# Attention and two expert layers on one core: zero products in TensorE's waits, other chunk widths, a mask copied by VectorE, pooled keys in a tile of their own, and a new written order

## The chip, the cores and the metric

The kernel runs on one core of one Trainium2 chip. The metric is the device time of one execution in microseconds (us). The times shown are the median of three runs and the three runs themselves; the profile is of a further execution with a time of its own.

## The reference, cut to what matters

Inputs are fp32: q, k and v of 2 x 8 heads, 576 positions, 64 wide. The output is 1152 x 512.

```python
def _attn_ref(q, k, v):
    ...
    q_d = q.reshape(B, H, Sd, factor, D).mean(axis=3)      # factor 4: 144 pooled positions; k_d, v_d alike
    ...
    out_d = sm_attn(q_d, k_d, v_d)
    out_up = np.repeat(out_d, factor, axis=2)
    mask = np.abs(pos[:, None] - pos[None, :]) < factor    # a band of 7 keys
    scores = np.where(mask, scale * np.matmul(q, k.transpose(0, 1, 3, 2)), -1000000000.0)
    ...                                                    # softmax
    return out_up + np.matmul(attn, v)

def _moe_ref(x, w_in, w_out):                              # 1152 x 512, 512 x 2048, 2048 x 512
    h = x @ w_in
    g = h * (1.0 / (1.0 + np.exp(-h)))
    return g @ w_out

def _moe2_ref(x, domain_probs, w1, w2):                    # 4 experts, 512 x 1024, 1024 x 512
    p = domain_probs / (domain_probs.sum(-1, keepdims=True) + 1e-09)
    for e in range(E):
        out += p[:, e:e + 1] * (np.maximum(x @ w1[e], 0.0) @ w2[e])
```

## The kernel before, in words

Every large product is made of three: each factor is split into a high part in TensorE's rounded fp32 format and a low part, and high x high, high x low and low x high are added in PSUM. So a weight passes through a raw tile (DMA), a high part (ScalarE) and a low part (GpSimd or VectorE) before TensorE may use it. The weights of the first layer come as pairs of 32-bit halves in 64-bit places: step A (L236, ScalarE) scales the upper halves into a tile `dec`, step B (L239, VectorE) or Z (L242, ScalarE) shifts the lower bits, step C (L244, VectorE) joins them, step w (L250, ScalarE) makes the high part and step L (L251, GpSimd) the low part. There are 8 units of 4 such pieces (A0 to A31 and so on); units 0, 1, 4, 5 are of w_in, 2, 3, 6, 7 of w_out.

Attention is cut into 16 jobs of two heads and 256 or 320 positions. The steps of job i are: S (local scores and the mask, L403 and L410, TensorE), x (maximum and subtraction, L418 and L419, VectorE), e (exponential, L424, ScalarE), D (pooled scores, L444 for jobs 0 to 3 and L448 for the others, TensorE), n and d (their maximum and exponential), u, r and g (sums, reciprocals and scaling), T (transpositions, L490 and L492, TensorE) and a (their copies, L493 to L500, ScalarE), V (values, L518 and L522, TensorE), o and f (both outputs joined), h and l (the split of x into xh and xl). The keys of the first four jobs are pooled by GpSimd (k, L342), in place; those of later jobs with their queries (p). The mask, two unit matrices and two zeroed tiles for queries are made by GpSimd at the start (`constants`).

The first layer follows: G steps (x times w_in) and H steps (times w_out), over four chunks of positions and two halves of the 2048 hidden columns. In the first half the chunks are 256, 320, 256 and 320 wide (`XN`), in the second 256, 256, 256 and 384. The first two chunks of the first half are computed in quarters, woven with attention (`quarter`); the first products of all are M0 to M3 (`start_mm`, L993). Then come the four experts.

Each engine works its list in order. The order of the attention and of most of the first layer is written out by hand for each engine in `WRITTEN` (step names in a row); what is not named there, all of the experts among it, is put in order by the framework's scheduler. All loads go out on SP's queue, also in written order. Eight transfers are under way at most: each later one waits for the one eight before it, or for its own tile to be free.

Of the kernel before, what the change touches and what calls it, by code (L numbers as in the profile page):

```python
# [22 lines left out]
NT = NB * S  # L23
# [31 lines left out]
LOW_ON_DVE = (0, 1, 2, 3)  # L55
# [7 lines left out]
def attention_moe_kernel(ctx, tc, kqa, kqb, qtl, va, vb, w64, w1d, w2d, dpr, out):  # L63
# [28 lines left out]
    const.tile([128, 16], F32, name="gap_w")  # L92
    prt = const.tile([128, 9, NE + 1], F32, name="pr")
# [132 lines left out]
    def split_raw(u, j, t):  # L226
        if u < 8:
# [4 lines left out]
            d = d_p.tile([128, 512], F32, tag="dec", name="dec")  # L232
# [19 lines left out]
        else:  # L252
# [5 lines left out]
            behind(ACT, ACT.activation(out=h[:, c], in_=t, func=ACTF.Copy))  # L258
            behind(DVE, DVE.tensor_tensor(out=l[:, c], in0=t, in1=h[:, c].bitcast(F32), op=ALU.subtract))
# [17 lines left out]
    def eye(t):  # L277
        return (POOL.memset(t, 0.0), POOL.affine_select(out=t, in_=t, compare_op=ALU.not_equal, fill=1.0, base=0,
                                                        pattern=[[-1, 128]], channel_multiplier=1))

    def constants():
        mark("cm", POOL.memset(mask, 0.0))
        for h in range(2):
            m = mask[64 * h:64 * h + 64]
            mark("cm", POOL.affine_select(out=m, in_=m, pattern=[[0, 6], [1, WIN]], compare_op=ALU.is_ge,
                                          fill=NEG, base=0, channel_multiplier=-1),
                 POOL.affine_select(out=m, in_=m, pattern=[[0, 6], [-1, WIN]], compare_op=ALU.is_ge,
                                    fill=NEG, base=6, channel_multiplier=1))
# [193 lines left out]
    def trans(j):  # L482
# [5 lines left out]
        j.at = ac.tile([WIN, 5, 128], F32, tag="at", name="at")  # L488
        for m in range(nb):
# [19 lines left out]
    def values(j):  # L509
# [3 lines left out]
        v = vd[b, hp]  # L513
        for h in range(2):
# [145 lines left out]
    def quarter(ci, p, o, n):  # L660
        c = slice(o, o + n)
        g = [4 * ci + i for i in range(4)]
        two = n == 256
# [9 lines left out]
        if two:  # L673
            b = [mm_tile() for _ in range(2)]
            groups = [[(d, half(b[d // 2], d % 2)) for d in range(4)]]
        else:
            groups = [[(d, mm_tile()) for d in ds] for ds in ((0, 1, 2), (3,))]
        step[0] -= 0.5
        for sums in groups:
            first = {}  # L680
            for i in range(4):
                wh, wl = parts(2 + p, i)
                for d, ps in sums:
                    if not two or len(sums) == 4:
                        next_step(0.125)
                    s = slice(d * 128, d * 128 + 128)
                    h, l = gh[g[i]][:, 0:n], gl[g[i]][:, 0:n]
                    for x, (a, y) in enumerate(((wh, h), (wh, l), (wl, h))):
                        z = two and d % 2
                        m = PE.matmul(out=ps[:, 0:n], lhsT=a[:, s], rhs=y, start=(not z and i == 0 and x == 0),  # L690
                                      stop=(i == 3 and x == 2), skip_group_check=True)
                        if i == 0 and x == 0:
                            first[d] = m
                            if z:
                                after(m, first[d - 1])
                        mark(f"H{ci}_{d}_{4 * p + i}", m)
                if i:
                    attn_tick()
            for d, ps in sums:
                ya = acc[:, d * NT + o:d * NT + o + n]  # L700
                if p == 0:
                    i = ACT.activation(out=ya, in_=ps[:, 0:n], func=ACTF.Copy, scale=0.5)
                else:
                    i = DVE.scalar_tensor_tensor(out=ya, in0=ps[:, 0:n], scalar=0.5, in1=ya, op0=ALU.mult, op1=ALU.add)
                mark(f"ya{ci}_{d}_{p}", i)
# [34 lines left out]
    def stage_ahead():  # L740
        while todo and not pieces:
# [156 lines left out]
    def outputs(e, ci, ch, p):  # L898
# [303 lines left out]
```

## Time and profile before

| | us |
|---|---|
| median of 3 runs | 652.15 |
| the three runs | 652.35, 652.15, 647.56 |
| the profiled execution, device time | 649.48 |
| its span, first to last instruction | 647.70 |

In the profile TensorE is busy for 629.0 us (97%), VectorE for 415.4, ScalarE for 325.3 and GpSimd for 249.1. A busy TensorE is not yet one at its peak: the granted clock and the number of matmuls in a stretch have to be read beside it. A matmul's own duration overlaps that of the next, so its cost in a stream is the stretch divided by the number of matmuls that begin in it. The time ahead of the first instruction and behind the last, 649.48 - 647.70 = 1.78 us, lies outside the span.

### The profile page before, as it was taken

What the parts mean: (1) busy time and instruction counts of PE and PEld (TensorE: products, weight loads), DVE (VectorE), ACT (ScalarE), POOL (GpSimd) and SP (SyncE); (2) the same over time, 40 slices, a digit from 0 to 9 for tenths busy, and PEclk for the clock granted to TensorE, in tenths of its full rate; (3) what the DMA queues carried; (4) which work ended last, traced back from release to release, by engine and by line L of the source; (5) the groups of instructions that cost most, each with busy time, mean ns of one, the idle gap of its engine ahead of it and who ended that gap; (6) DMA issues with size and microseconds to landing.
All of it is one profiled execution on the core that took longest, in us unless ns stands there. A gap on an engine that the chain in (4) does not pass through costs nothing.

```text
span 647.7 us, 13723 instructions
## 1 busy us (share of the span) xinstructions
PE 629.0 (97%) x5492; PEld 617.6 (95%) x5492; DVE 415.4 (64%) x859; ACT 325.3 (50%) x746; POOL 249.1 (38%) x353
## 2 busy tenths in 40 slices
PE   4989999999999999999999999999999999999995
PEld 3779999999999999999999999999999999999995
DVE  5878676547445737756668954769855579755534
ACT  2788776578725525443346533355533366433321
POOL 7567532034400004443646412654433564333210
PEclk9789999999999999999999999999999999999998
DMA  8955551235600400420013300024200020001001
GB/s 276 285 164 187 175 173 56 78 100 163 194 2 1 132 1 1 162 67 2 1 34 108 113 9 1 1 67 131 66 1 2 1 66 1 1 33 35 2 32 50
DMA packets 16928, 48.17 MB, mean 74 GB/s; under 512 B 2976, under 2 KB 4256, under 8 KB 16864
## 3 DMA queue, kind: packets, MB, share of 16 engines
q1 hardware_dynamic: 16864, 47.29, 23.4%
q8 instruction: 43, 0.70, 0.5%
q14 instruction: 21, 0.17, 0.1%
HBM read 44.93 MB, written 2.36 MB: 73 GB/s over the span
## 4 chain that ended last, share of the span: by engine, by line
PE 94%; DVE 3%; ACT 2%; DMA 1%; issue 0%; POOL 0%; ACTq 0%
PE mm L603 57%; PE p L864 27%; PE mm L690 4%; PE s L403 2%; PE o L522 1%; PE t L490 1%; PE o L518 1%; DVE acc L892 1%; DMA kq<-in_kqa_dram 1%; PE mm L993 1%; PE s L410 1%; PE s L448 0%; PE t L492 0%; ACT dec L236 0%; PE mm L403 0%
## 5 line engine op out<-in xcount | busy, mean ns | idle before, releaser
L603 PE MATMUL mm<-xh,wbuf 128*128 128x256 f32 (+2 forms) x1248 | 259.6, 292 | 0.0
L603 PEld LDWEIGHTS mm<-xh,wbuf 128*128 128x128 f32 x1248 | 203.7, 188 | 0.1
L603 PE MATMUL mm<-xl,wbuf 128*128 128x256 f32 (+2 forms) x624 | 182.0, 292 | 0.0
L849 POOL TENSOR_TENSOR r<-r 128x128 f32<-128x128 f32 x160 | 95.0, 606 | 177.4 <-ACT r L843 133.1
L852 DVE TENSOR_TENSOR h<-r,h 128x384 fp32r<-128x384 f32 (+1 forms) x128 | 91.6, 718 | 65.7 <-ACT h L851 65.4
L851 ACT ACTIVATE h<-r 128x384 fp32r<-128x384 f32 (+1 forms) x128 | 73.3, 578 | 93.5 <-POOL r L849 54.5
L603 PEld LDWEIGHTS mm<-xl,wbuf 128*128 128x128 f32 x624 | 117.1, 188 | 0.0
L864 PE MATMUL p<-wext,h 128*128 128x256 f32 x672 | 89.2, 276 | 0.0
L864 PE MATMUL p<-wbuf,h 128*128 128x256 f32 x672 | 82.7, 276 | 0.0
L864 PEld LDWEIGHTS p<-wext,h 128*128 128x128 f32 x672 | 82.2, 188 | 0.0
L864 PEld LDWEIGHTS p<-wbuf,h 128*128 128x128 f32 x672 | 79.4, 188 | 0.0
L603 PE MATMUL mm<-gh,wbuf 128*128 128x256 f32 (+2 forms) x384 | 77.1, 292 | 0.0
L603 PEld LDWEIGHTS mm<-gh,wbuf 128*128 128x128 f32 x384 | 62.0, 188 | 0.0
L843 ACT ACTIVATE r<-mm 128x512 f32<-128x512 f32 x48 | 28.6, 596 | 65.4 <-PE mm L603 64.7
L849 DVE TENSOR_TENSOR r<-r 128x128 f32<-128x128 f32 x96 | 39.3, 410 | 34.0 <-ACT r L843 29.4
L603 PE MATMUL mm<-gl,wbuf 128*128 128x256 f32 (+2 forms) x192 | 55.8, 291 | 0.0
L631 DVE TENSOR_TENSOR gl<-gf,gh 128x256 fp32r<-128x256 f32 (+2 forms) x64 | 34.2, 540 | 18.1 <-ACT gh L630 17.7
L625 DVE SCALAR_TENSOR_TENSOR gf<-th,mm 128x256 f32<-128x256 f32 (+2 forms) x64 | 28.7, 451 | 23.6 <-ACT th L624 21.6
L251 POOL TENSOR_TENSOR wbuf<-dec,wbuf 128x512 fp32r<-128x512 f32 x24 | 31.0, 1301 | 26.4 <-ACT wbuf L250 20.4
L892 DVE SCALAR_TENSOR_TENSOR acc<-p,pr,acc 128x256 f32<-128x256 f32 (+1 forms) x63 | 36.1, 605 | 3.6 <-PE p L864 3.0
L794 POOL TENSOR_TENSOR wext<-kst,wext 128x512 fp32r<-128x512 f32 x8 | 10.4, 1300 | 69.5 <-ACT wext L792 46.9
L630 ACT ACTIVATE gh<-gf 128x256 fp32r<-128x256 f32 (+2 forms) x64 | 28.0, 442 | 16.5 <-DVE gf L625 15.7
(173 smaller groups left out, 1035.2 us busy)
## 6 DMA issues: line engine op xcount, KB each, us to landing
stg<-in_w_dram SPq DMA_DIRECT2D x29, 512.0 KB
kst<-in_w2d_dram SPq DMA_DIRECT2D x16, 512.0 KB
kst<-in_w1d_dram SPq DMA_DIRECT2D x12, 512.0 KB
kq<-in_kqb_dram SPq DMA_DIRECT2D x8, 323.0 KB
kq<-in_kqa_dram SPq DMA_DIRECT2D x6, 419.0 KB
stg<-in_w1d_dram SPq DMA_DIRECT2D x4, 512.0 KB
acc<-in_w_dram SPq DMA_DIRECT2D x3, 512.0 KB
vw<-in_vb_dram SPq DMA_DIRECT2D x8, 180.0 KB
```

Of the source, the lines that this page charges most:

```text
L251: mark(f"L{4 * u + j}", POOL.tensor_tensor(out=l, in0=d, in1=h.bitcast(F32), op=ALU.subtract))
L603: ins = [PE.matmul(out=ps, lhsT=l, rhs=r, start=(first and i == 0), stop=(last and i == n - 1)) for i, (l, r) in enumerate(pairs)]
L625: mark(f"gf{c}_{ft}", DVE.scalar_tensor_tensor(out=gf[:, 0:n], in0=th[:, 0:n], scalar=1.0, in1=ps[:, 0:n], op0=ALU.add, op1=ALU.mult))
L630: latest[ACT] = mark(f"gh{c}_{ft}", ACT.activation(out=gh[g][:, 0:n], in_=gf[:, 0:n], func=ACTF.Copy))
L631: latest[DVE] = mark(f"gl{c}_{ft}", DVE.tensor_tensor(out=gl[g][:, 0:n], in0=gf[:, 0:n], in1=gh[g][:, 0:n].bitcast(F32), op=ALU.subtract))
L690: m = PE.matmul(out=ps[:, 0:n], lhsT=a[:, s], rhs=y, start=(not z and i == 0 and x == 0), stop=(i == 3 and x == 2), skip_group_check=True)
L843: ACT.activation(out=r[:, 0:4].rearrange("p s t -> p (s t)"), in_=ps[:, 0:512], func=ACTF.Relu)
L849: latest[eng] = eng.tensor_tensor(out=r[:, o], in0=r[:, a], in1=r[:, b], op=op)
L851: ACT.activation(out=h, in_=r[:, part], func=ACTF.Copy)
L852: latest[DVE] = DVE.tensor_tensor(out=l, in0=r[:, part], in1=h.bitcast(F32), op=ALU.subtract)
L864: ins = [PE.matmul(out=ps, lhsT=x, rhs=y, start=(opens and k == 0 and i == 0), stop=(k == 3 and i == n - 1), skip_group_check=True) for i, ...
L892: DVE.scalar_tensor_tensor(out=o, in0=ps, scalar=p, in1=o, op0=ALU.mult, op1=ALU.add)
```

## The change

- Matmuls on a tile of zeros (128 x 128 weights, 256 columns, bf16) are put ahead of three steps of TensorE: 3 ahead of S0, 11 ahead of T1 and 3 ahead of T2. They write a PSUM tile that the step then overwrites.
- The first half has the chunks of the second: 256, 256, 256, 384. The quarters keep their width of 256, and the code for 320 is gone. The tiles for 384 are opened ahead of the last chunk of the first half.
- One sixth of the mask is made by GpSimd on 70 columns; VectorE copies it to the others. The zeroing of the mask, unit matrices and query tiles goes from GpSimd to VectorE.
- The keys of jobs 0 to 3 are pooled through a tile `ktmp` and no longer in place.
- Step Z of units 4 to 7 (16 pieces) becomes step B on VectorE, and `dec` of these pieces lies in place in the raw tile.
- All five written orders are new and reach further, to chunk 5 and the first weights of the experts.

```diff
-XN = (256, 320, 256, 320)
-CHUNKS = (tuple(zip(XOFF, XN)), ((0, 256), (256, 256), (512, 256), (768, 384)))
+CHUNKS = ((0, 256), (256, 256), (512, 256), (768, 384))
+FILL = {"S0": 3, "T1": 11, "T2": 3}
-LOW_ON_DVE = (0, 1, 2, 3)
+LOW_ON_DVE = (0, 1, 2, 3) + tuple(range(16, 32))
+    ktmp = const.tile([128, SD, 2], F32, name="ktmp")
...
-            d = d_p.tile([128, 512], F32, tag="dec", name="dec")
+            d = d_p.tile([128, 512], F32, tag="dec", name="dec") if u < 4 else v[:, :, 1].bitcast(F32)
...
+    zeros = acc[:, 4470:4598].bitcast(BF16)
+
+    def fill(name, t):
+        for _ in range(FILL.get(name, 0)):
+            mark(name, PE.matmul(out=t, lhsT=zeros[:, 0:128], rhs=zeros, start=True, stop=True, skip_group_check=True))
+
     def constants():
-        mark("cm", POOL.memset(mask, 0.0))
+        mark("cw", DVE.memset(zeros, 0.0))
+        m1 = mask[:, 1]
+        mark("zcm", DVE.memset(m1, 0.0))
         for h in range(2):
-            m = mask[64 * h:64 * h + 64]
-            mark("cm", POOL.affine_select(out=m, in_=m, pattern=[[0, 6], [1, WIN]], compare_op=ALU.is_ge,
...
+            m = m1[64 * h:64 * h + 64]
+            mark("cm", POOL.affine_select(out=m, in_=m, pattern=[[1, WIN]], compare_op=ALU.is_ge, fill=NEG, base=0,
...
+        mark("cM", DVE.tensor_copy(out=mask[:, 0], in_=m1),
+             DVE.tensor_copy(out=mask[:, 2:6], in_=m1.unsqueeze(1).to_broadcast([128, 4, WIN])),
+             DVE.memset(mask[:, 0, 0:3], NEG), DVE.memset(mask[:, 5, WIN - 3:WIN], NEG))
...
-            mark(f"k{j.i}", fold(k4), padd(kd[j.b, j.hp], k4[:, :, 0], k4[:, :, 1]))
+            mark(f"k{j.i}", padd(ktmp, k4[:, :, 0:2], k4[:, :, 2:4]), padd(kd[j.b, j.hp], ktmp[:, :, 0], ktmp[:, :, 1]))
...
+            if hf == 0 and lastc:
+                m1ctx.close()
+                open_g(384)
...
-        """in_kq0 in_kq1 in_s0 in_kq2 in_vg0 in_kq3 in_vg1 in_kq4 in_kq5 in_vw0 in_s1 in_qt in_vg3 in_vw1 in_s3 in_vg2 in_vw2
+        """in_kq0 in_kq1 in_s0 in_vg0 in_s1 in_kq4 in_kq2 in_vg1 in_vw0 in_kq5 in_kq3 in_s2 in_vw1 in_qt in_vw2 in_s3 in_vg2
...
-        """S0 S1 D0 D1 S2 S3 T0 D2 S4 V0 S5 T1 D3 D5 D4 V1 M0 T2 M1 V2 T3 tD S6 T4 V3 D6 S7 M2 tT M3 V4 T5 D7 S8 T6 V5 D8
+        """S0 S1 D0 D1 T0 S4 S2 V0 S5 D2 S3 T1 D5 V1 D3 D4 T2 M0 T3 V2 M1 tD S6 T4 V3 D6 M2 S7 tT M3 V4 S8 T5 D7 H0_0_0
...
```

TensorE, from the first pooled scores (D0 and D1, L444) to the first values. Before:

```order
L444 MATMUL s<-kd,qp 64x144 x4
L403 MATMUL mm<-kq_f 64x70 x8
L410 LDWEIGHTS ident_103
L410 MATMUL mm<-mask,ident_103 128x280
L403 MATMUL mm<-acc 64x70 x8
L410 LDWEIGHTS ident_103
L410 MATMUL mm<-mask,ident_103 128x280
L490 MATMUL t_309<-ident,sm 70x128 x4
L492 MATMUL t_310<-ident,ed 72x128 x2
L444 MATMUL mm<-kd,qp 64x144 x2
L403 MATMUL s<-kq 64x70 x10
```

In the changed kernel (L415 and L422 are S, L456 is D, L503 and L505 are T, L532 and L536 are V):

```order
L456 MATMUL s<-kd,qp 64x144 x4
L503 MATMUL t_316<-ident,sm 70x128 x4
L505 MATMUL t_317<-ident,ed 72x128 x2
L415 MATMUL s<-kq 64x70 x10
L422 LDWEIGHTS ident_104
L422 MATMUL s<-mask,ident_104 128x350
L415 MATMUL mm<-kq_f 64x70 x8
L422 LDWEIGHTS ident_104
L422 MATMUL mm<-mask,ident_104 128x280
L532 MATMUL o<-atd_326,vd 64x64 x4
L536 MATMUL o<-at,vw 64x64 x8
```

The scores of jobs 2 and 3 (into `mm`) stood ahead of the first transposition; now T0 comes straight behind D1, S4 and S2 follow, and S3 stands behind V0, S5 and D2.

TensorE, from the last of the 11 zero products (L286) ahead of T1 to the values of job 1 and the next pooled scores, in the changed kernel:

```order
L286 LDWEIGHTS acc
L286 MATMUL t_386<-acc 128x256
L503 MATMUL t_386<-ident,sm 70x128 x4
L505 MATMUL t_387<-ident,ed 72x128 x2
L460 MATMUL s<-kd,qbd_107 128x144
L532 MATMUL o<-atd_407,vd 64x64 x4
L536 MATMUL o<-at,vw 64x64 x8
L456 MATMUL mm<-kd,qp 64x144 x2
L460 MATMUL s<-kd,qbd_106 128x144
```

Ten more such pairs stand ahead of the first row, and S3 ahead of them.

ScalarE, from its start. Before:

```order
L424 ACT_TABLE_LOAD
L424 ACTIVATE s<-s 128x280
L236 ACTIVATE dec<-stg_136 128x512
L424 ACTIVATE s<-s 128x280
L465 ACTIVATE ed,s<-s,stf 128x144 x2
L424 ACTIVATE mm<-mm 128x280
L480 ACTIVATE ed<-ed,stf 128x144
L493 ACTIVATE at<-t_309 70x512
```

In the changed kernel (L436 is e, L477 is d, L492 is g, L506 is a):

```order
L307 ACT_TABLE_LOAD
L307 ACTIVATE qdl<-zero 128x128
L436 ACTIVATE s<-s 128x280
L477 ACTIVATE ed,s<-s,stf 128x144
L436 ACTIVATE s<-s 128x280
L236 ACTIVATE dec<-stg_140 128x512
L492 ACTIVATE ed<-ed,stf 128x144
L236 ACTIVATE dec<-stg_142 128x512
L477 ACTIVATE ed,s<-s,stf 128x144
L250 ACTIVATE wbuf<-dec 128x512
```

The table load stood with the first exponential, behind that one's wait; it now stands with a copy of zeros (step tab). The scaling of job 0 (g, L492) no longer stands behind the exponential of job 2, and the second weight piece (L236) has come forward.

ScalarE, at the last weight pieces of the first layer, in the changed kernel (L638 is the tanh of a G step, L644 the high part of its result, L250 the high part of a weight):

```order
L644 ACTIVATE gh_2310<-gf 128x256
L250 ACTIVATE wbuf<-stg_2547 128x512
L638 ACTIVATE th<-mm 128x256 x2
L250 ACTIVATE wbuf<-stg_2587 128x512
L644 ACTIVATE gh_2308<-gf 128x256
L250 ACTIVATE wbuf<-stg_2554 128x512
L644 ACTIVATE gh_2306<-gf 128x256
```

These are w29, w31 and w30 among the last steps of chunk 4's G; before, all of w28 to w31 stood ahead of that chunk's second tanh.

## Rows read from the trace of the kernel before

**Rows 1.** The profile's first part: busy time of each engine.

```profile
PE 629.0 (97%) x5492; PEld 617.6 (95%) x5492; DVE 415.4 (64%) x859; ACT 325.3 (50%) x746; POOL 249.1 (38%) x353
```

**Rows 2.** Busy time by stretch: stretch and length, engines, TensorE's granted clock, DMA.

```profile
15.00:20.00 5.00, 3.96 (x41) 2.88 (x43) 3.84 (x12) 2.28 (x6) 2.13 (x6) 0.64 0.97 278
20.00:25.00 5.00, 4.51 (x54) 3.63 (x52) 3.89 (x10) 3.33 (x11) 2.49 (x7) 0.68 0.97 300
30.00:35.00 5.00, 4.43 (x89) 3.60 (x90) 4.61 (x12) 5.00 (x12) 2.63 (x4) 1.00 0.39 110
35.00:40.00 5.00, 3.71 (x39) 3.32 (x35) 3.82 (x13) 4.44 (x15) 3.58 (x8) 0.69 0.59 178
100.00:180.00 80.00, 79.96 (x692) 78.82 (x692) 44.54 (x94) 56.17 (x132) 22.59 (x22) 1.00 0.36 112
200.00:640.00 440.00, 440.00 (x3580) 440.00 (x3579) 284.49 (x539) 191.08 (x400) 164.67 (x230) 1.00 0.13 39
```

**Rows 3.** TensorE's waits: for whom, us in total, times, longest.

```profile
PE s L403 <- DMA kq<-in_kqa_dram: 4.4, 1, 4.4
PE t L490 <- DVE sm L478: 1.9, 1, 1.9
...
PE s L448 <- ACT s L424: 0.5, 1, 0.5
```

**Rows 4.** Stretches of one width: 256, 320, 384 columns; TensorE busy, clock, DMA.

```profile
186.27:188.99 2.72, 2.72 (x26) 1.00 0.00 0
149.77:152.85 3.08, 3.08 (x23) 1.00 0.82 253
244.80:247.92 3.12, 3.12 (x19) 1.00 0.00 0
```

**Rows 5.** TensorE in order of time: start, us, instruction, [idle before <- whom].

```profile
4.37 1.20 PE L403 MATMUL s<-kq 64*64 64x70 f32 x16 [4.37 <-DMA kq<-in_kqa_dram]
...
20.97 1.43 PE L403 MATMUL s<-kq 64*64 64x70 f32 x20
...
26.15 0.39 PE L993 MATMUL mm<-xh,wbuf 128*128 128x256 f32 x1
...
31.90 0.83 PE L403 MATMUL s<-kq 64*64 64x70 f32 x20
...
36.53 0.49 PE L448 MATMUL s<-kd,qbd 128*128 128x144 f32 x2 [1.29 <-DVE st L472]
...
42.79 0.76 PE L522 MATMUL o<-at,vw 70*64 70x64 f32 x20
```

**Rows 6.** ScalarE in order of time.

```profile
6.97 1.28 ACT L424 ACT_TABLE_LOAD   x1 [6.97 <-DVE s L419]
...
29.49 0.42 ACT L480 ACTIVATE ed<-ed,stf 128x144 f32<-128x144 f32 x1
...
34.48 0.61 ACT L250 ACTIVATE wbuf<-dec 128x512 fp32r<-128x512 f32 x1
...
35.99 0.45 ACT L424 ACTIVATE s<-s 128x350 f32<-128x350 f32 x1
```

**Rows 7.** SP's queue in order of time: when these loads were issued.

```profile
5.35 0.35 SPq L128 DMA_DIRECT2D vw<-in_va_dram  x1
...
13.64 0.30 SPq L128 DMA_DIRECT2D vg_f<-in_va_dram  x1
14.73 0.30 SPq L128 DMA_DIRECT2D vw_f<-in_va_dram  x1
```

**Rows 8.** GpSimd in order of time.

```profile
9.96 1.04 POOL L342 TENSOR_TENSOR vg_f<-vg_f 72x512 f32<-72x512 f32 x1 [1.52 <-DMA vg_f<-in_va_dram]
...
172.44 2.54 POOL L251 TENSOR_TENSOR wbuf<-dec,wbuf 128x512 fp32r<-128x512 f32 x2 [1.58 <-ACT wbuf L250]
```

**Rows 9.** VectorE in order of time: step B twice.

```profile
10.04 1.24 DVE L239 TENSOR_SCALAR stg<-stg 128x512 int32<-128x512 int32 x1
...
22.04 0.42 DVE L239 TENSOR_SCALAR stg<-stg 128x512 int32<-128x512 int32 x1
```

More of the change, by code (lines that the diff above doesn't have):

```diff
@@ L257, in split_raw @@
             c = slice(j * 1024, (j + 1) * 1024)
-            behind(ACT, ACT.activation(out=h[:, c], in_=t, func=ACTF.Copy))
-            behind(DVE, DVE.tensor_tensor(out=l[:, c], in0=t, in1=h[:, c].bitcast(F32), op=ALU.subtract))
+            mark(f"hw{u}_{j}", ACT.activation(out=h[:, c], in_=t, func=ACTF.Copy))
+            mark(f"lw{u}_{j}", DVE.tensor_tensor(out=l[:, c], in0=t, in1=h[:, c].bitcast(F32), op=ALU.subtract))
     actx = ExitStack()
@@ L672, in quarter @@
         flush()
[L673 to L677, printed above, removed]
-        step[0] -= 0.5
[L679 to L705, printed above, removed]
@@ new lines, in quarter @@
+        b = [mm_tile() for _ in range(2)]
+        sums = [half(b[d // 2], d % 2) for d in range(4)]
+        step[0] -= 0.5
+        first = {}
+        for i in range(4):
+            wh, wl = parts(2 + p, i)
+            for d, ps in enumerate(sums):
+                next_step(0.125)
+                s = slice(d * 128, d * 128 + 128)
+                h, l = gh[g[i]], gl[g[i]]
+                for x, (a, y) in enumerate(((wh, h), (wh, l), (wl, h))):
+                    m = PE.matmul(out=ps, lhsT=a[:, s], rhs=y, start=(d % 2 == 0 and i == 0 and x == 0),
+                                  stop=(i == 3 and x == 2), skip_group_check=True)
+                    if i == 0 and x == 0:
+                        first[d] = m
+                        if d % 2:
+                            after(m, first[d - 1])
+                    mark(f"H{ci}_{d}_{4 * p + i}", m)
+            if i:
+                attn_tick()
@@ L707, in g2_evac @@
+        for d, ps in enumerate(sums):
+            ya = acc[:, d * NT + o:d * NT + o + n]
+            if p == 0:
+                i = ACT.activation(out=ya, in_=ps, func=ACTF.Copy, scale=0.5)
+            else:
+                i = DVE.scalar_tensor_tensor(out=ya, in0=ps, scalar=0.5, in1=ya, op0=ALU.mult, op1=ALU.add)
+            mark(f"ya{ci}_{d}_{p}", i)
     def g2_evac(hf, db, c, ps, n):
@@ L966, in attention_moe_kernel @@
-        g15 o14 h14 gh2_2 a15 th2_3 th2_4 gh2_4 o15 Z20 gh2_3 th2_5 w17 gh2_5 h15 th2_6 w16 Z19 th2_7 gh2_6 A18 A19 gh2_7
-        w19 w18 ya2_1 ya2_0 A20 ya2_2 Z22 w20 A21 th3_0 gh3_0 A22 th3_1 Z21 w21 gh3_1 th3_2 Z23 A23 gh3_2 ya2_3 th3_3 w23
-        th3_4 gh3_3 Z25 gh3_4 w22 th3_5 A24 Z24 th3_6 gh3_5 A25 th3_7 w25 w24 gh3_7 Z26 gh3_6 A26 A27 Z27 w26 w27 Z28
-        ya3_0 A28 ya3_1 A29 Z29 w28 ya3_2 w29 Z30 A30 Z31 A31 th4_0 w30 w31 th4_1 ya3_3 gh4_0 gh4_1 th4_2 th4_3 gh4_2
-        gh4_3 th4_4 th4_5 gh4_4 gh4_5 th4_6 gh4_6 th4_7 gh4_7 yh4_0 yh4_1 yh4_2 yh4_3""",
@@ new lines, in attention_moe_kernel @@
+        o12 e14 A18 gh1_6 e15 th1_7 a13 gh1_7 h12 d14 th2_0 d15 th2_1 g14 o13 a14 gh2_1 h13 gh2_0 th2_2 th2_3 g15 o14
+        gh2_2 h14 th2_4 th2_5 gh2_3 gh2_4 a15 th2_6 gh2_5 th2_7 o15 gh2_7 gh2_6 w16 w17 h15 w18 ya2_1 ya2_0 A19 w19 A20
+        ya2_2 A21 ya2_3 th3_0 w20 w21 th3_1 gh3_0 gh3_1 A22 th3_2 th3_3 A23 gh3_2 gh3_3 w22 th3_4 A24 th3_5 gh3_4 gh3_5
+        w23 th3_6 th3_7 gh3_6 w24 gh3_7 A25 w25 A26 ya3_0 w26 A27 ya3_2 ya3_1 A28 w27 w28 th4_0 gh4_0 A29 th4_1 th4_2
+        ya3_3 gh4_1 gh4_2 th4_3 A30 th4_4 A31 gh4_3 gh4_4 th4_5 gh4_5 w29 th4_6 th4_7 w31 gh4_6 w30 gh4_7 yh4_1 hw8_1
@@ L989, in start_mm @@
             hold.extend(mm_tile() for _ in range(2))
+            fill("M0", hold[0][:, 0:256])
         for i in range(4):
```

145 lines of the change are left out of this document (77 added, 68 removed).

## The prediction

> **What bounds the kernel now.** I read the busy times of the engines first, then the stretches, TensorE's waits, and last its list and ScalarE's in order of time. TensorE is busy for 629.0 us of the 647.7 us span [rows 1]. That alone does not say that it is the bound, since a matmul's duration overlaps the next. The stretches do: from 200 to 640 us it is busy for 440.00 of 440.00 us at a granted clock of 1.00 [rows 2]. In pure stretches 24 matmuls of 256 columns begin in 2.72 us, 21 of 320 in 3.08 and 18 of 384 in 3.12 (the rows count one or two more that began earlier) [rows 4]: 113.3, 146.7 and 173.3 ns each. These are stream costs with no wait in them. In such stretches only fewer or cheaper matmuls save time, and no reordering of the other engines does.
>
> What can be had lies in the first 50 us. TensorE waits there eight different ways, 11.9 us in all, from 4.4 us for the first keys down to 0.5 [rows 3]. The first 4.4 stay, since no order brings the first keys sooner; 7.5 us are open. The second loss is the clock, which has two levels, 1.2 and 2.4 GHz. It was 0.64 in the mean from 15 to 20 us, 0.68 from 20 to 25 and 0.69 from 35 to 40, with 3.96, 4.51 and 3.71 us busy [rows 2]. If a share s of a stretch is at the low level, the mean is 1 - s/2, so s is 0.72, 0.64 and 0.62, and half of what was busy at that level is lost: 1.4 + 1.4 + 1.2 = 4.0 us. No low clock is recorded before 15 us, but 16 score matmuls took 1.20 us at 4.37 us and 20 took 1.43 at 20.97, against 0.83 for 20 at 31.90 [rows 5]: the first 12 us run at the slow rate too, and four such score steps lose about 1.20 - 0.66 each, 2.2 us. In all 7.5 + 4.0 + 2.2 = 13.7 us could come back, no more.
>
> **The change, part by part.**
>
> *Widths.* The first half has 4 x 192 matmuls (96 for G and 96 for H in each chunk). Two chunks of 320 become one of 256 and one of 384: 192 x 113.3 + 192 x 173.3 - 384 x 146.7 ns = 21.8 + 33.3 - 56.3 = **-1.3 us**, all in the stretch where TensorE is the bound. The reopening of the tiles at 384 moves one chunk forward; before, the same step between the halves cost TensorE no wait, as the eight rows of waits leave none after the first 50 us [rows 3].
>
> *The first transposition.* ScalarE's table load of 1.28 us began at 6.97, behind the first maxima [rows 6]. Now it runs at the start with the copy of zeros, while the keys are on their way. With the scores of jobs 2 and 3 out of the way as well, T0 can end before 12 us. But then the loads decide. Before, a load is issued as soon as the one eight places ahead has landed: kq1, 838 KB into the list, at 5.35 us, and kq4 at 13.64 and kq5, 3410 KB into it, at 14.73 [rows 7], so 274 KB per us. By that rate and the new list kq4 (2473 KB) lands at 11.4, kq2 (2892) at 12.9, kq5 (3647) at 15.6 and kq3 (4066) at 17.1 us. S5, 1.43 us without its mask product, S3, 1.20 without its own, and D2 stand between V0 and the zero products; laid end to end at the slow rate from V0's end, which I put at 16.4, they end near 20.1 (an estimate). So much of what T0 gained is spent on later keys, because the weights s0 and s1 went ahead of them.
>
> *Zero products.* The 3 ahead of S0 fall into the 4.37 us wait for keys. The 3 ahead of T2 cost 3 x 0.113 = 0.3 us at the full rate. The 11 ahead of T1 stand behind S3, and T1's inputs are ready by then: 1.2 us at the full rate, 2.5 at half, and they are on the path. They are repaid if the clock rises by them: in 15 to 25 us TensorE stayed at the low level for 0.72 x 3.96 + 0.64 x 4.51 = 5.7 busy us on small matmuls alone [rows 2]. I take 2.0 us, half of them at either level, and T1 done at 22.6. V1, D3, D4 and T2 follow through ScalarE's copies, and M0 starts near 25.7 us against 26.15 [rows 5]: **-0.4 us**. This is the whole gain up to there.
>
> *From M0 to D6.* D6 ran at 36.53, behind the exponential of job 6, which ScalarE reached at 35.99 [rows 5, 6]. ScalarE was the bound there: busy 5.00 of 5.00 us from 30 to 35 [rows 2]. Before, 13 steps stood between its step at 29.49 (g3) and that exponential, among them pieces 2 of A and w (w2, 0.61 us at 34.48). Now T3 comes straight behind M0, so g3 can end at 28.4 instead of 29.9, and 11 steps follow, about 0.6 us less: A2 and w2 have come ahead, one Z step (Z10) has gone behind, d5 has moved in. The exponential then ends near 34.5 and D6 starts at 34.6: **-1.9 us**, with the 0.4 in it.
>
> *From D6 to the end of V4* (42.79 + 0.76 = 43.55 [rows 5]). TensorE had the low clock here for 0.62 x 3.71 = 2.3 busy us [rows 2]. With M2 ahead of S7 and shorter waits I take the clock as full: **-1.1 us**. Later only one wait of under a microsecond is left, which I do not count.
>
> *The mask, the zeroing and `ktmp`.* GpSimd is done with the mask earlier and may pool the first keys when they land, not when S0 has read them. D0 waits for the exponential anyway, so this is worth nothing by itself. If VectorE's copies came late, S0 would slip behind 4.37 us, at most by a few tenths.
>
> *Step B for Z.* Sixteen pieces cost VectorE 16 x 0.42 = 6.7 us [rows 9]. From 100 to 180 us it is busy 44.5 of 80 us, ScalarE 56.2 [rows 2], so VectorE has room, and ScalarE gets some. One row warns: B took 1.24 us at 10.04, three times as long, while GpSimd's sum at 9.96 ran for 1.04 [rows 8, 9]. At that price 16 steps cost 19.8 us, which still fits into 35 us idle. The Trainium skill, SBUF — State Buffer, section "Who interferes with whom", has a rule that speaks against moving work from ScalarE to VectorE beside GpSimd: a VectorE instruction in a two-port mode and a GpSimd instruction exclude each other for the whole of the later one's wait, and ScalarE never waits. By that rule both engines lose up to one GpSimd step per piece; the row of 1.24 us agrees. It matters only if late pieces hold up TensorE, which is the rival below.
>
> *The experts* keep their order: the last 2505 rows of TensorE's list are the same. Their waits are none [rows 2].
>
> **The sum.** 649.48 - 1.3 - 1.9 - 1.1 = 645.2 us, against the profiled execution. That one lies 2.7 us below the median of the runs shown and 0.9 below the mean of all four executions (650.4). Put among such runs I expect **646 us**, and between 643.5 and 648.5 if this case holds.
>
> **The rivals.**
>
> *The loads set the pace.* From 15 to 25 us the DMA engines are busy 0.97 of the time [rows 2], and the bytes needed before M0 are much the same. For it: my own reckoning gives only 0.4 us up to M0. Against it: the gain I count is behind that, where ScalarE is the bound. If it holds, only the widths gain, and the 11 products may cost up to 2.5 us: 648.2 to 650.7.
>
> *The zero products lift the clock for good and the order closes the waits.* Then half or more of the 13.7 us comes back: 649.48 - 1.3 - 7 = 641.2, at best 649.48 - 1.3 - 13.7 = 634.5. For it: 5.7 us of slow work in one place. Against it: the keys still land at 17.1 us.
>
> *Slower: the last weights of the first layer come late.* Before, GpSimd had finished the last low part by 174.98 us [rows 8]. Now a raw tile is freed only when GpSimd has read it, a hold longer by a w (0.61) and an L step (1.27), 1.9 us on each of 16 pieces in three tiles: about 10 us for the last. On top, w29 to w31 stand among chunk 4's last G steps on ScalarE, where 14 H steps of 3 x 113.3 ns, 4.8 us, stand on TensorE between the last G step and the first that needs w30's piece, and two w and two L steps alone take 2 x 0.61 + 2 x 1.27 = 3.8. Every piece that two engines lock each other for comes later by about 1 us, and each wait is paid in full, since TensorE is the bound there. It decides once the pieces are more than 1 us later than that; at its full 10 us the time is 645.2 + 10 = 655. Against it: neither VectorE nor ScalarE is short of time there [rows 2].
>
> **Chances.** Forecast 0.52; loads set the pace 0.23; clock and waits repaired 0.13; slower 0.12. The range takes in the first two with half of each of the others: 640.5 to 652. A measurement of this kernel can tell about 1% from no change, here 6.5 us, so faster by over 1% means below 645.6: the third case and some six tenths of the first, 0.43. Slower by over 1% (above 658.7) needs the last case at its worst or one that I do not see: 0.06. The rest, 0.51, is within 1%.
>
> **What would show it.** T0 before 12 us and S3 behind kq3's landing near 17; the granted clock above 0.9 from 20 to 25 and from 35 to 40 us; M0 near 25.7; the exponential of job 6 before 35 us and V4 done near 40.5; the three widths in the first half at 113 and 173 ns; no wait of TensorE after 60 us. I am wrong if M0 comes well before 24 us (the loads were no bound), if the clock stays low behind the 11 products, or if TensorE shows waits at the H steps of chunk 4.

## The result, and the profile after

The changed kernel takes 656.1 us (median of 6 runs, 655.4 to 659.6), the kernel before 650.3 in the runs beside it (6 runs, 647.0 to 652.4): 1.010 times as long, with a 95% interval of 1.006 to 1.014. I had put it at 646 us and the range at 640.5 to 652. The profiled execution took 656.03 us, its span is 654.2.

First the busy times of the changed kernel, which answer to [rows 1]:

```profile
PE 639.8 (98%) x5509; PEld 629.1 (96%) x5509; DVE 420.7 (64%) x885; ACT 315.4 (48%) x730; POOL 247.6 (38%) x346
```

TensorE is busy for 10.8 us more, though it waits less. Its waits, against [rows 3]:

```profile
PE s L286 <- DVE acc L289: 3.3, 1, 3.3
PE s L456 <- ACT s L436: 2.4, 1, 2.4
PE o L532 <- ACT atd L513: 0.5, 1, 0.5
...
```

With four more of 0.4, 0.3, 0.2 and 0.2 they sum to 7.3 us against 11.9, and all of them lie in the first 45 us: there is none at the last weights of the first layer. The stretches, against [rows 2] (same columns):

```profile
15.00:20.00 5.00, 5.00 (x65) 4.02 (x66) 3.45 (x10) 2.42 (x7) 3.20 (x5) 1.00 0.91 281
20.00:25.00 5.00, 4.51 (x62) 3.97 (x62) 4.43 (x13) 2.50 (x8) 3.64 (x10) 1.00 0.93 246
...
35.00:40.00 5.00, 5.00 (x66) 4.67 (x68) 4.48 (x14) 5.00 (x16) 2.52 (x5) 1.00 0.93 267
100.00:180.00 80.00, 80.00 (x654) 79.41 (x654) 46.41 (x104) 45.82 (x110) 20.02 (x15) 1.00 0.30 90
200.00:640.00 440.00, 440.00 (x3480) 440.00 (x3479) 278.76 (x524) 185.02 (x388) 164.06 (x230) 1.00 0.12 38
```

In the rows from 20 and 35 us the clock is 1.00 where it was 0.68 and 0.69. The 1.00 of the first row says only that no low clock is recorded there: the 20 score matmuls of S5 still took 1.43 us at 18.01, as many 0.83 at 32.08 (rows in the section on the prediction), so TensorE ran at the low rate up to about 21.5 us. The loss stands in the last row: from 200 to 640 us TensorE is busy for all 440.00 us at a clock of 1.00, as before, but begins 3480 matmuls and not 3580. It does not wait, and it is not throttled; its matmuls are dearer. Pieces of one kind show it. In the changed kernel, 72 matmuls of 256 columns in the first layer, then 45 in the experts (21 products with w2 and 24 with w1), then 24 of 384:

```profile
177.14:185.30 8.16, 8.16 (x74) 8.16 (x73) 3.59 (x7) 2.48 (x7) 4.18 (x3) 1.00 0.58 185
...
301.99:307.29 5.30, 5.30 (x47) 5.30 (x46) 2.10 (x5) 1.75 (x3) 0.57 (x1) 1.00 0.00 0
...
325.44:329.60 4.16, 4.16 (x27) 4.16 (x25) 0.99 (x2) 1.69 (x4) 1.34 (x2) 1.00 0.01 2
```

That is 113.3 ns in the first layer, as in [rows 4], but 5.30 / 45 = 117.8 ns in the experts; the 384 wide ones here are at the old 173.3. So a 256-column matmul costs 4.4 ns more. DMA is idle in that row and ScalarE and VectorE have little to do.

I measure the **expert stage** from its first product out of `wext` to the start of its last group of products. It holds the same 2928 matmuls in the same order in both kernels and in every experiment. Before:

```profile
278.26:633.13 354.87, 354.87 (x2930) 354.87 (x2929) 231.81 (x441) 153.50 (x319) 145.95 (x211) 1.00 0.11 34
```

After:

```profile
273.80:639.53 365.73, 365.73 (x2931) 365.73 (x2930) 232.43 (x440) 153.49 (x319) 144.91 (x211) 1.00 0.10 32
```

The stage begins 4.46 us earlier and lasts 10.86 us longer; behind it lie 14.67 us against 14.57. -4.46 + 10.86 + 0.10 = 6.5 us, which is the difference of the spans (654.2 - 647.7). The whole question is the 10.86.

### The profile page after: what moved, and what is told of

The parts are those of the page before. It is cut to its first block, busy times and chain, and to the rows that moved or that the text cites. A ratio compares the mean times of both kernels' runs of the same rounds, so it can differ in the third digit from the quotient of the medians.

```text
span 654.2 us, 13782 instructions
## 1 busy us (share of the span) xinstructions
PE 639.8 (98%) x5509; PEld 629.1 (96%) x5509; DVE 420.7 (64%) x885; ACT 315.4 (48%) x730; POOL 247.6 (38%) x346
## 4 chain that ended last, share of the span: by engine, by line
PE 93%; DVE 3%; ACT 1%; DMA 1%; issue 1%; SPq 0%; POOL 0%; ACTq 0%; POOLq 0%; DVEq 0%
PE mm L617 57%; PE p L873 27%; PE mm L698 3%; PE s L415 1%; DMA stg<-in_w_dram 1%; PE o L536 1%; PE t L503 1%; PE o L532 1%; DVE acc L901 1%; PE mm L1011 0%; PE s L422 0%; PE s L460 0%; DVE s L439 0%; PE mm L415 0%; PE t L505 0%
## 5 line engine op out<-in xcount | busy, mean ns | idle before, releaser
L617 PE MATMUL mm<-xh,wbuf 128*128 128x256 f32 (+1 forms) x1248 | 264.7, 295 | 0.0
L617 PE MATMUL mm<-xl,wbuf 128*128 128x256 f32 (+1 forms) x624 | 183.8, 294 | 0.0
L617 PE MATMUL mm<-gh,wbuf 128*128 128x256 f32 (+1 forms) x384 | 79.2, 296 | 0.0
L858 DVE TENSOR_TENSOR r<-r 128x128 f32<-128x128 f32 x96 | 33.6, 350 | 38.7 <-ACT r L852 34.1
L617 PE MATMUL mm<-gl,wbuf 128*128 128x256 f32 (+1 forms) x192 | 56.7, 296 | 0.0
L639 DVE SCALAR_TENSOR_TENSOR gf<-th,mm 128x256 f32<-128x256 f32 (+1 forms) x64 | 28.7, 450 | 21.7 <-ACT th L638 20.8
L645 DVE TENSOR_TENSOR gl<-gf,gh 128x256 fp32r<-128x256 f32 (+1 forms) x64 | 31.9, 506 | 13.7 <-ACT gh L644 13.2
L638 ACT ACTIVATE th<-mm 128x256 f32<-128x256 f32 (+1 forms) x64 | 26.0, 408 | 26.3 <-PE mm L617 26.1
L617 PEld LDWEIGHTS mm<-gl,wbuf 128*128 128x128 f32 x192 | 36.0, 188 | 0.0
L644 ACT ACTIVATE gh<-gf 128x256 fp32r<-128x256 f32 (+1 forms) x64 | 27.7, 441 | 13.8 <-DVE gf L639 13.8
```

The lines of the kernel that those rows point to most:

```text
L617: ins = [PE.matmul(out=ps, lhsT=l, rhs=r, start=(first and i == 0), stop=(last and i == n - 1)) for i, (l, r) in enumerate(pairs)]
L638: mark(f"th{c}_{ft}", ACT.activation(out=th[:, 0:n], in_=ps[:, 0:n], func=ACTF.Tanh, scale=0.5))
L639: mark(f"gf{c}_{ft}", DVE.scalar_tensor_tensor(out=gf[:, 0:n], in0=th[:, 0:n], scalar=1.0, in1=ps[:, 0:n], op0=ALU.add, op1=ALU.mult))
L644: latest[ACT] = mark(f"gh{c}_{ft}", ACT.activation(out=gh[g][:, 0:n], in_=gf[:, 0:n], func=ACTF.Copy))
L645: latest[DVE] = mark(f"gl{c}_{ft}", DVE.tensor_tensor(out=gl[g][:, 0:n], in0=gf[:, 0:n], in1=gh[g][:, 0:n].bitcast(F32), op=ALU.subtract))
L858: latest[eng] = eng.tensor_tensor(out=r[:, o], in0=r[:, a], in1=r[:, b], op=op)
```

## The experiments

**What could it be.** `ktmp`, 1152 bytes in each partition, was put into `const` behind `gap_w`. Whatever is allocated behind it on that side moves up by 1152 bytes: `pr`, `wext` (the weights of one unit of the first layer, then of half the w2 pieces), `u5` (another unit) and `ks` (sums for w2). `wbuf`, `xh`, `xl`, `h`, `gh` and `gl` stay. That is theory A. The rivals: something in the new lists (B), or the zero products (C), carries on into the experts. No experiment but those on the zero products adds, drops or reorders an instruction.

**`ktmp` elsewhere.**

```diff
-    ktmp = const.tile([128, SD, 2], F32, name="ktmp")
+    ktmp = first_p.tile([128, SD, 2], F32, name="ktmp")
```

> The changed kernel with one tile elsewhere: ktmp (1152 bytes per partition) lies among the first jobs' tiles at the other end of the memory, so that pr, wext and ks are back at the addresses of the kernel before; no instruction's order changes. Theory A (the experts' matmuls are dearer because wext, ks and pr lie 1152 bytes higher): a 256-column matmul of the experts costs 113.3 ns again everywhere, the expert stage gets its 10.9 us back, and the time is 656.1 - 10.9 = 645.2 us. Theory B (what the change does to the lists of the engines or to the zero products carries on into the experts): 117.7 ns as in the changed kernel and 656 us. In both, the first values of chunk 0 end near 40.5 us.

Measured: 644.73 us (6 runs), 0.994 times the time before (interval 0.992 to 0.996). Its expert stage, and the 45 matmuls of above:

```profile
274.00:628.87 354.87, 354.87 (x2930) 354.87 (x2929) 231.34 (x441) 153.49 (x319) 146.49 (x211) 1.00 0.11 34
...
301.20:306.30 5.10, 5.10 (x48) 5.10 (x46) 2.10 (x5) 1.76 (x3) 0.58 (x1) 1.00 0.00 0
```

354.87 us again, 113.3 ns again. Theory A holds, B falls.

**The shift alone, in the kernel before.**

```diff
     const.tile([128, 16], F32, name="gap_w")
+    const.tile([128, 288], F32, name="gap_k")
```

> The kernel before with an unused tile of 1152 bytes per partition between gap_w and pr, where ktmp stands in the changed kernel; nothing else. Theory A: the expert stage costs 10.9 us more, products from wext take 117.7 ns each all the time, and the time is 650.3 + 10.9 = 661 us. Theory B: 113.3 ns and 650 us, since no instruction is changed.

Measured: 659.96 us (4 runs), 1.018 (1.015 to 1.021). An unused tile costs as much as the whole loss:

```profile
276.98:642.71 365.73, 365.73 (x2930) 365.73 (x2929) 232.43 (x440) 153.49 (x319) 144.76 (x211) 1.00 0.10 32
```

**Without zero products, and a longer shift.**

```diff
-FILL = {"S0": 3, "T1": 11, "T2": 3}
+FILL = {}
```

> The changed kernel without its 17 zero products, ktmp left where it is. Theory A: the expert stage stays at 117.7 ns; only the start changes: the 11 products in front of T1 took 1.4 us there, and if the clock is up without them the start is 1.2 us shorter (655), if the clock falls as in the kernel before, 1 to 3 us longer (657 to 659). Theory C (the zero products shift TensorE's instruction stream or leave a state behind that makes each later matmul dearer): 113.3 ns in the experts and about 645 us.

Measured: 656.84 us (4 runs), expert stage 365.72. C falls.

```diff
     ktmp = const.tile([128, SD, 2], F32, name="ktmp")
+    const.tile([128, 224], F32, name="gap_k")
```

> The changed kernel with 896 bytes of unused tile behind ktmp, so that pr, wext and ks lie 2048 bytes higher than in the kernel before instead of 1152. If it is the address within some power of two up to 2048 bytes that matters (theory A, first form): 113.3 ns in the experts and 645 us. If any shift against the tiles that stay (wbuf, xh, xl, h) breaks a fit (second form), or under theories B and C: 117.7 ns and 656 us.

Measured: 644.65 us (10 runs), 0.994 (0.992 to 0.996), expert stage 354.88. A shift is not bad in itself; its size counts.

**Which tile.** From here on most kernels ran once, with the profile, and what is read is the length of the expert stage in it; kernels that should agree in it do so to 0.01 us. Four kernels made from e1_ktmp_right:

```diff
-        b, o = (wext[0], 48 + 2 * KF * k) if k < 2 else (wbuf, 48 + 2 * UW * (k - 2))
+        b, o = (wext[0], 80 + 2 * KF * k) if k < 2 else (wbuf, 48 + 2 * UW * (k - 2))
```

> e1_ktmp_right with the w2 products' weights of the pieces k = 0 and 1 laid 128 bytes further inside wext (offset 80 instead of 48 columns of fp32); no tile moves. 128 bytes is what is left of the 1152 once whole 1024s are taken off. Theory W (what counts is where the weights that stream from wext lie): the expert stage, from the first product out of wext to the end of the last, is 365.7 us instead of 354.9. Theories K (ks) and R (pr): 354.9 us.

Measured: expert stage 365.73.

```diff
         wext.append(late.tile([128, 4 * KF + 128], F32R, name="wext"))
+        late.tile([128, 288], F32, name="gap_k")
```

> e1_ktmp_right with an unused tile of 1152 bytes behind wext, so that ks (and u5, used in the first layer) lies 1152 bytes higher, wext and pr where they were. Theory K (the sums in ks, which VectorE and GpSimd write and read beside TensorE): expert stage 365.7 us. Theories W and R: 354.9 us.

Measured: 366.72. Both theories that I had set against each other got their number, or nearly, so my reading that one tile is to blame was wrong.

```diff
     const.tile([128, 16], F32, name="gap_w")
+    const.tile([128, 32], F32, name="gap_k")
```

> e1_ktmp_right with 128 bytes of unused tile between gap_w and pr: pr, wext and ks all 128 bytes higher. If the address counts within 1024 bytes or less, 128 is the same as 1152: expert stage 365.7 us. If 1152 was bad only as a distance of its own (within 2048 bytes), it is 354.9 or a third value.

Measured: 365.73, the same as 1152 bytes.

```diff
     const.tile([128, 16], F32, name="gap_w")
+    const.tile([128, 288], F32, name="gap_k")
     prt = const.tile([128, 9, NE + 1], F32, name="pr")
+    const.tile([128, 224], F32, name="gap_p")
```

> e1_ktmp_right with 1152 unused bytes ahead of pr and 896 behind it: pr lies 1152 bytes higher, wext and ks 2048 bytes, which cost nothing in e4_shift_2048. Theory R (pr, which VectorE reads at each sum of the outputs): expert stage 365.7 us. Theories W and K: 354.9 us.

Measured: 354.87; `pr` is out of it.

**`ks` for one expert, and the period.** e9_ks_first_only opens `ks` for expert 0 behind a gap of 1152 bytes and closes it again; e10 to e12 are e7 with 256, 128 and 64 columns of fp32 for its 32.

```diff
-                ks_p.append(ctx.enter_context(tc.tile_pool(name="ks", bufs=2)))
+                k0.enter_context(tc.tile_pool(name="gap_k", bufs=1)).tile([128, 288], F32, name="gap_k")
+                ks_p.append(k0.enter_context(tc.tile_pool(name="ks0", bufs=2)))
...
     for k in range(2, 4):
         split_kk(0, k)
+    k0.close()
+    ks_p[0] = ctx.enter_context(tc.tile_pool(name="ks", bufs=2))
```

> e1_ktmp_right with ks 1152 bytes higher for the four pieces of expert 0 alone (its sums and splits, from about 248 to 273 us); all later sums lie where they lay, and so do wext, pr and u5. Theory S (the access to a badly placed tile only tips TensorE into a dearer pace, which then lasts by itself): 256-column matmuls at 117.7 ns also between 281 and 305 us, where no engine touches ks, and an expert stage well above 354.9 us, up to 366.7 as in e6_ks_shifted. Theory D (each access to a badly placed tile costs directly, while it lasts): at most 0.5 us more, 355.4 us.

> e1_ktmp_right with 1024 unused bytes between gap_w and pr: pr, wext and ks all 1024 bytes higher. 128 and 1152 bytes gave 365.73 us for the expert stage to the hundredth, 2048 gave 354.88. If the fit repeats every 1024 bytes or less, 354.9 us; if only every 2048, something else, probably 365.7.

> The same with 512 bytes. If the fit repeats every 512 bytes or less: 354.9 us. If only every 1024 or 2048: about 365.7 us.

> The same with 256 bytes. If the fit repeats every 256 bytes: 354.9 us. If only every 512 or more: about 365.7 us.

Measured, expert stage: e9 354.87, e10 354.87, e11 354.88, e12 354.88. 256 bytes and its multiples are free, 128 and 1152 are not. And moving `ks` for expert 0 costs nothing, so in e6 it was hardly `ks`. What e6 moved besides is `u5`, which TensorE reads up to about 247 us and never again. Compare e6, in a stretch behind that:

```profile
283.60:300.00 16.40, 16.40 (x142) 16.40 (x141) 8.87 (x17) 5.56 (x10) 5.18 (x9) 1.00 0.00 1
```

with e9, the same stretch:

```profile
283.60:300.00 16.40, 16.40 (x147) 16.40 (x146) 9.01 (x17) 5.54 (x10) 5.18 (x9) 1.00 0.01 2
```

In both kernels every engine reads and writes the same places here (none touches `ks` in this stretch), and e6 begins 142 matmuls where e9 begins 147. The difference must come from before.

**TensorE's own reads.** Again on e1_ktmp_right, `u5` alone, then the w2 weights of one piece alone:

```diff
-            wext.append(u5_p[0].enter_context(tc.tile_pool(name="u5", bufs=1)).tile([128, 2 * UW], F32R, name="u5"))
-        return (wext[s - 4], 0) if s > 3 else (wbuf, 2 * UW * s)
+            wext.append(u5_p[0].enter_context(tc.tile_pool(name="u5", bufs=1)).tile([128, 2 * UW + 32], F32R, name="u5"))
+        return (wext[s - 4], 32 * (s == 5)) if s > 3 else (wbuf, 2 * UW * s)
```

> e1_ktmp_right with the weights in u5 (one unit of the first layer's second half, read by TensorE up to about 247 us and never again) 128 bytes higher; wext, ks, pr and every tile of the experts stay. Theory S' (TensorE itself tips into the dearer pace when its weights come from a badly placed tile, and keeps it after the tile is done with): 256-column matmuls at 117.7 ns from 248 us on, expert stage about 366.7 us as in e6_ks_shifted. Theory D (only accesses while they last): 354.9 us.

Measured: 48 matmuls of 256 columns with `u5`'s weights and the 96 with `wbuf`'s behind them, 48 of 384 with `u5`'s and the 96 behind those, a stretch of 256 columns after that, and the expert stage:

```profile
218.20:223.64 5.44, 5.44 (x51) 5.44 (x50) 3.50 (x10) 2.95 (x9) 0.00 (x0) 1.00 0.02 5
223.64:234.51 10.87, 10.87 (x98) 10.87 (x97) 3.83 (x10) 2.37 (x6) 0.00 (x0) 1.00 0.01 2
242.84:251.16 8.32, 8.32 (x50) 8.32 (x49) 5.27 (x9) 3.98 (x8) 0.99 (x1) 1.00 0.00 0
251.16:267.93 16.77, 16.77 (x98) 16.77 (x98) 12.48 (x19) 5.75 (x11) 10.81 (x12) 1.00 0.17 64
268.00:276.00 8.00, 8.00 (x70) 8.00 (x69) 6.80 (x9) 6.17 (x13) 4.54 (x5) 1.00 0.75 262
...
277.11:643.83 366.72, 366.72 (x2930) 366.72 (x2929) 233.09 (x440) 153.47 (x319) 144.18 (x211) 1.00 0.10 32
```

366.72 us, as e6 to the hundredth, from 128 bytes in a tile that is done with at 251 us in this run; so `ks`, which e6 moved for all experts, adds nothing. While `u5` is read nothing is paid (5.44 / 48 = 113.3 ns, 8.32 / 48 = 173.3), and in the chunks of 256 columns nothing behind it either (10.87 / 96 = 113.2). Only behind its last use, at 384 columns, does the dear pace set in (16.77 / 96 = 174.7), and it stays to the end of the kernel: from 268 us 68 matmuls of 256 columns take 8.00 us, 117.6 ns each (the row counts two that began earlier). In the changed kernel, too, matmuls with `wext` and `u5` are read at 113.3 ns, and the dear pace sets in behind the last of `u5`, at 247.85 us.

```diff
-        b, o = (wext[0], 48 + 2 * KF * k) if k < 2 else (wbuf, 48 + 2 * UW * (k - 2))
+        b, o = (wext[0], 48 + 32 * (k == 1) + 2 * KF * k) if k < 2 else (wbuf, 48 + 2 * UW * (k - 2))
```

> e1_ktmp_right with the w2 weights of piece k = 1 alone 128 bytes further inside wext; those of k = 0 and all else stay. Theory S': the products of k = 1 tip TensorE and the matmuls behind them, out of tiles that were not moved, cost 117.7 ns as well: nearly all of e5_w2_offset's 10.9 us, an expert stage of 363 to 366 us. Theory D: only the matmuls of k = 1 are dearer, about 4 x (3 x 21 + 33) = 384 at 4.4 ns, 1.7 us: 356.6 us.

Measured:

```profile
272.43:631.58 359.15, 359.15 (x2931) 359.15 (x2929) 232.18 (x441) 153.49 (x319) 145.94 (x211) 1.00 0.10 33
...
375.26:380.56 5.30, 5.30 (x48) 5.30 (x46) 1.78 (x3) 1.93 (x4) 1.60 (x3) 1.00 0.01 3
...
391.16:396.27 5.11, 5.11 (x48) 5.11 (x46) 2.10 (x5) 1.66 (x4) 0.57 (x1) 1.00 0.02 5
```

4.28 us more, between the two theories. The last two rows are 45 matmuls each out of tiles that were not moved: one at 117.8 ns, the other at 113.6. The dear pace outlasts its cause here too, but ends after a while.

**Place or distance.** A last pair moves all that TensorE reads, by 128 and by 64 bytes modulo 256 (e18 has 16 and 72 for 32 and 56):

```diff
-    ctx.enter_context(tc.tile_pool(name="gap_r", bufs=1, side="right")).tile([128, 24], F32, name="gap_r")
+    ctx.enter_context(tc.tile_pool(name="gap_r", bufs=1, side="right")).tile([128, 56], F32, name="gap_r")
...
+    const.tile([128, 32], F32, name="gap_k")
     xh = const.tile([128, HP, NT], F32R, name="xh")
```

> e1_ktmp_right with every tile that TensorE reads 128 bytes from where it lay, modulo 256: 128 unused bytes ahead of xh, and 128 more at the other end. In all fast kernels so far weights start at 192 and streamed operands at 128 modulo 256 (wbuf, wext and u5 against xh, xl, gh and gl in the first layer; h against the w2 weights in the experts); now it is 64 and 0. If the distance between the two counts (64 modulo 256), the expert stage stays at 354.9 us; if the places themselves count, it rises, by about 11 us or more (365.7).

> The same by 64 bytes: weights start at 0 and streamed operands at 192 modulo 256, the distance again 64. If the distance counts: 354.9 us. If the places count: dearer, about 365.7 us or another value; 64 bytes has not been tried.

Measured: expert stage 354.88 and 354.87. The row of e17:

```profile
275.30:630.18 354.88, 354.88 (x2931) 354.88 (x2930) 231.35 (x441) 153.47 (x319) 146.51 (x211) 1.00 0.11 33
```

So it is not the place as such; what counts is how the operands lie to each other. Start addresses in a partition, modulo 256 (worked out from the order and the sizes of the tiles; no trace holds addresses):

| kernel | matmuls with another distance than 64 | weights, streamed | expert stage, us |
|---|---|---|---|
| before, e1, e4, e8 to e12, e15, e16 (below) | none | 192, 128 | 354.87 or 354.88 |
| e17; e18 | none | 64, 0; 0, 192 | 354.88; 354.87 |
| changed, e2, e3, e7 | G steps from `wext`, `u5`; w2 products from `wext` | 64, 128; 192, 0 | 365.73 (e3 365.72) |
| e5 | w2 products from `wext` | 192, 0 | 365.73 |
| e14 | those of k = 1 | 192, 0 | 359.15 |
| e6, e13 | G steps from `u5` | 64, 128 | 366.72 |

Every kernel with 64 throughout is cheap, every one with 192 anywhere is dear. But every dear kernel mixes the two, and the price does not follow the single matmul: in e13 those at 192 cost 113.3 ns and later ones at 64 cost 117.7. No kernel has 192 throughout, so whether 192 itself is dear, or the change from one distance to the other, is not shown.

**The repair, and what the zero products are worth.**

```diff
     ktmp = const.tile([128, SD, 2], F32, name="ktmp")
+    const.tile([128, 32], F32, name="gap_k")
```

> The changed kernel, ktmp where it is, with 128 unused bytes behind it, so that pr, wext and ks lie 1280 = 5 x 256 bytes higher than in the kernel before. By e10, e11 and e12 a shift by a multiple of 256 bytes is free: expert stage 354.9 us, time 645 us, faster than the kernel before by some 0.5%.

> e15_gap_128 without its 17 zero products: what they are worth with the experts at their old pace. If they lift the clock in time, the kernel without them is slower, by the 1.1 us by which the expert stage began later in e3_no_zero_products than in the changed kernel (646); if they only cost what they take on the path, it is 1 us faster (644).

Measured: e15 644.98 us (11 runs), 0.994 (0.991 to 0.997), expert stage 354.87; e16 645.31 us (12 runs), 0.993 (0.991 to 0.996). The changed kernel with 128 unused bytes beats the kernel before by 0.6%, and the zero products make no difference that can be measured. In e16's profile the clock is up without them:

```profile
20.00:25.00 5.00, 4.36 (x50) 3.71 (x50) 4.86 (x14) 3.64 (x12) 4.15 (x7) 1.00 1.04 277
```

In e3's it is not, in the same stretch:

```profile
20.00:25.00 5.00, 3.27 (x38) 2.35 (x38) 4.86 (x13) 3.77 (x11) 4.48 (x9) 0.88 0.97 269
```

The two kernels have the same instructions in the same order, so the start differs by 3 us from execution to execution: M0 came at 23.29 us in e16, at 26.41 in e3. One profile of it tells little.

## Why the prediction was wrong, point by point

**The failed step** is "The experts keep their order: the last 2505 rows of TensorE's list are the same. Their waits are none." Both halves came true. What I took from them, that the stage lasts as long, did not: 365.73 us for 354.87. I had taken 113.3 ns as the cost of a 256-column matmul and asked only how many there are; and I had put `ktmp` at nothing ("worth nothing by itself") by what reads and writes it, not by what lies behind it. The diff showed it in one line, and the kernel's unused tiles `gap`, `gap_w`, `gap_r` and `gap_h` were a hint that places matter. None of my rivals covered it: my slower case was late weights. Without these 10.86 us the time would lie inside the range.

The start, from the changed kernel's profile against [rows 5]:

```profile
4.42 1.20 PE L415 MATMUL s<-kq 64*64 64x70 f32 x16 [0.33 <-DMA kq<-in_kqa_dram]
...
11.89 1.04 PE L503 MATMUL t<-ident,sm 128*70 128x128 f32 x4 [0.44 <-DVE sm L490]
12.72 0.64 PE L505 MATMUL t<-ident,ed 128*72 128x128 f32 x2
...
18.01 1.43 PE L415 MATMUL s<-kq 64*64 64x70 f32 x20
...
21.57 1.36 PE L286 MATMUL t<-acc 128*128 128x256 bf16 x11
22.77 0.60 PE L503 MATMUL t<-ident,sm 128*70 128x128 f32 x4
...
26.82 0.37 PE L1011 MATMUL mm<-xh,wbuf 128*128 128x256 f32 x1
...
32.08 0.83 PE L415 MATMUL s<-kq 64*64 64x70 f32 x20
...
34.98 0.36 PE L460 MATMUL s<-kd,qbd 128*128 128x144 f32 x1 [0.20 <-ACT s L436]
...
39.76 0.76 PE L536 MATMUL o<-at,vw 70*64 70x64 f32 x20
```

- *First transposition.* T0 was to end before 12 us; it began at 11.89 and ended at 12.72 + 0.64 = 13.36. D1 ahead of it had waited 2.4 us for the exponential of job 1, which in the new list stands behind d0, itself waiting for VectorE; I had not followed that chain. The table load was out of the way, at the head of ScalarE's list (against [rows 6]):

```profile
0.74 1.28 ACT L307 ACT_TABLE_LOAD   x1 [0.74 <-PEq L1209]
...
34.40 0.45 ACT L436 ACTIVATE s<-s 128x350 f32<-128x350 f32 x1
```

- *From there to M0.* -0.4 us was forecast, +0.7 came: M0 at 26.82. S3 made way at 21.57, not at 20.1, since V0 had ended at 18.0 and not 16.4. The 11 products cost 22.77 - 21.57 = 1.2 us, all at the high clock level, where I had 2.0. So the clock had risen ahead of them; they took 1.20 us in all 16 kernels that have them, and my reason for them, that the clock would rise by them, is shown in none. In number the rival "the loads set the pace" is nearer here, but TensorE waited for no load behind 4.42 us. One execution does not decide this: with the same instructions up to there M0 came between 23.82 us (e10) and 27.05 (e13), as the low rate ended sooner or later (20 score matmuls of S5 took 0.83 us at 16.27 in e10, 1.43 at 18.48 in e13).
- *From M0 to D6.* The exponential of job 6 began at 34.40 and D6 at 34.98; 34.6 was forecast. The term of -1.9 measured -1.6.
- *D6 to V4.* V4 ended at 39.76 + 0.76 = 40.52, against 40.5 forecast and 43.55 before: -1.5 us for this part, where I had -1.1, at a clock of 1.00 as assumed.
- *Widths.* (The quarters of the second chunk were 320 wide before, not 256.) From V4's end to the experts it was 234.71 us and is 233.28, with 0.46 us of the dear pace in it already (96 matmuls of 384 in 16.76 us where e1 has 16.64, 78 of 256 in 9.19 where it has 8.85). That leaves -1.9: the -1.3 of the widths and the one wait of 0.65 us behind V4, at 47.99, that I did not count.
- *Sum up to the experts.* -4.3 forecast, -4.46 measured. With the experts at their old pace the same change gives 645.0 us in e1's profiled execution, where the sum said 645.2, and the median of e15's 11 runs is 644.98. That the profiled start fits to 0.2 us is in part luck: with the same instructions, and at the old pace, the expert stage began between 271.81 us (e11) and 275.34 (e18).
- *The slower rival.* GpSimd's last low part ended at 182.08 us and not 174.98 [rows 8], 7.1 us later where I gave it about 10. No matmul waited for it.
- *Step B.* The fear of 1.24 us a piece was unfounded:

```profile
L239 DVE TENSOR_SCALAR stg<-stg 128x512 int32<-128x512 int32 x19 | 8.6, 457 | 13.4 <-DMA stg<-in_w_dram 13.3
```

  457 ns in the mean is near the 0.42 us that I took [rows 9]. The rule of the Trainium skill, SBUF — State Buffer, "Who interferes with whom", that I had set against it shows little here.

## What to carry to other kernels

A new tile moves every tile behind it. Before an edit is costed at nothing where the instruction order is unchanged, compare the start addresses of TensorE's operands in both programs; if they moved against each other, the old cost of a matmul is no longer evidence. And when TensorE shows no wait and a full clock but fewer matmuls per stretch, measure one kind of matmul in several places: that separates a dearer matmul from more work. To test it, add unused bytes to the fast kernel, which changes nothing else.

## What the runs showed of the hardware that I had not expected

- In this kernel (fp32 data in TensorE's rounded format, weights 128 x 128) the pace of a stream of matmuls depends on how far their weights lie from the streamed operands in a partition, modulo 256 bytes: 113.3 ns for 256 columns where all are at 64, 117.7 where some matmuls at 192 have set the pace. Other distances, and 192 throughout, were not tried. For 384 columns it is 173.3 against 174.7 to 176.5 ns.
- The dear pace lasts. In e13 matmuls at 192 were read without a price (113.3 ns), and those behind them, at 64, cost 117.7 for 380 us. In e5 and e14 the price sets in with the products at 192 themselves. In the changed kernel it ends for about 16 us in each of the first three experts (325.44 to 329.60 above is part of the first), in e14 more often, in e13 never. What tips it and what ends it is open.
- It is TensorE's own: ScalarE's time in the expert stage is 153.49 us in the changed kernel and in e1, and `ks`, which VectorE, GpSimd and ScalarE use, changed nothing where it lay 1152 bytes higher (e9 for expert 0; e6 is as dear as e13, which left it in place). The Trainium skill, SBUF — State Buffer, section "SBUF: two separate sides", states that TensorE waits for no other engine at its ports. That agrees. Of TensorE's own two read ports the page says, in "Who interferes with whom", that they are independent; here the cost changes with how the two operands lie to each other (354.87 against 365.73 us), and the measurement decides.
